# The last fill unit in the scores' banks, the last reciprocal ahead of a weight piece, the last output in halves

## The chip, the core and the metric

One core of one Trainium2 chip runs the whole program. The metric is the time of an execution on the device in microseconds (us), as the median of several runs. TensorE (PE, with its weight loads as PEld), VectorE (DVE), ScalarE (ACT) and GpSimd (POOL) each work through a list of instructions in order; SyncE (SP) issues most of the loads and stores. Engines wait for one another by semaphores alone.

## The reference, cut to what matters

Three blocks follow one another in float32: soft-capped attention, a gated MLP with a spatial gate, and an MLP with a convolution gate.

```python
# attention: B, H, S, D = 2, 12, 448, 64
scores = cap * np.tanh(scale * q @ k.T / cap)
attn = np.exp(scores - max) / (sum + 1e-09)
x = attn @ v                               # to (B, S, 768)
# gated MLP: 768 -> 1024 -> 768
h = gelu(x @ w_in); u, v = h[..., :512], h[..., 512:]
v_s = w_sg @ layernorm(v, g_ln) + b_sg     # over the sequence
x = x + (u * v_s) @ w_out
# convolution gate: 768 -> 1024 -> 768, three taps along the sequence
h = relu(x @ w2_in)
out = (h * sigmoid(conv3(h, conv_w))) @ w2_out
```

## The kernel before, in words

Everything is held transposed: features on the 128 partitions, the 448 positions of a batch along the free side. A product is kept near float32 by splitting both factors into a high and a low part and issuing three matmuls (hi·hi, hi·lo, lo·hi) per tile of 128 features; `mm3` (L110) does this, so a unit over 6 feature tiles is 18 matmuls.

**Attention** (L286) runs over 12 head pairs N in two halves each, so over rounds R of 0 to 26. A round issues scores into four PSUM banks (tile "sc" of the pool `psa`), tanh and exp on ScalarE, and with a lag the products with V and the sums of the exponentials into three banks (tile "pv", named `sums`). That makes seven of the eight banks; the eighth belongs to the pool `psm`, whose one tile "mo" everything shares that takes turns there. All of attention's matmuls go through `ordered` (L383), which pins each behind the one before, so their order is that of the code. `pin(lasta)` and `pin(lastv)` do the same on ScalarE and VectorE for the instructions that use them. Everything else is put in order by a scheduler that is given the program in the order of the code.

**Fill units.** The next stage begins with u units: unit (b, i) is 128 features of x @ w_in for batch b, then a gelu (`gelu`, L221: a square on ScalarE, L223; L226 on VectorE; a tanh on ScalarE, L227; L230 on VectorE, which is the last to read the bank). The first four, of batch 0, are issued inside attention where TensorE would wait: the table `FILL` (L38) says in which round, L637 to L647 issue them. The first takes turns in rounds 15 to 23, the others come whole in rounds 24, 25 and 26. Units 0, 2 and 3 lie in the bank of `psm`; unit 1 lies in bank 1 of a tile "fi" (L642), which takes the four score banks when no more scores are to come.

**The last head pair.** `norm_pe` (L582) divides the last pair by its sums without a round trip through memory: ScalarE copies products and sums out of the banks (L586), VectorE adds a guard (L588) and inverts 224 columns (L589). A step later `spread` (L591) repeats the inverted sums over the partitions with four matmuls (eight passes in the trace, "pv<-E,sel"), VectorE multiplies (L599), and the result is split into X.

**Weights** come as pieces of float64. A piece in attention is loaded by SP, ScalarE or VectorE turns its top words into `hd` (L151, L153), VectorE joins them with the low words (L156), makes the high part (L162) and subtracts it to get the low part (L165). Pieces of later stages go through L181 and L184 on ScalarE, L191 and L194 on VectorE, then L198 and L203; the buffer of a piece is loaded again when its L203 is done.

**The next stage** (`rest`, L728) opens a pool `ps1` of seven banks in the place of the scores' and products' banks. Its units are numbered n: 0 to 3 are the fill units, 4 to 6 v units of batch 0 (matmuls L772 to L774, 512 columns, each followed by a gelu and a layer norm), 7 to 10 u units of batch 1, 11 to 14 v units, 15 to 22 the spatial gate (its product is read by L823, "gt", and split to GH and gl), 23 to 34 the output product. `bank(n)` (L751) says which pool a unit's bank comes from: n below 4 and every fourth from `psm`, the others from `ps1`. The last stage has 16 h units and then 12 output units: `f_unit` (L946) sums 24 matmuls in a bank, ScalarE copies it to `o` with the factor 0.5 (L952) and SP stores it (L953).

Of the kernel before, what the change touches and what calls it, by code (L numbers as in the profile page):

```python
# [9 lines left out]
F32 = mybir.dt.float32  # L10
# [5 lines left out]
AF = mybir.ActivationFunctionType  # L16
ALU = mybir.AluOpType
PSUM = bass.MemoryType.PSUM

P = 128  # L20
B, H, S, D = 2, 12, 448, 64
NPAIR = H // 2
DM, DF, DH = 768, 1024, 512
NK = DM // P
# [3 lines left out]
HS = S // 2  # L28
# [25 lines left out]
def stages(  # L54
# [17 lines left out]
    nc = tc.nc  # L72
    V, A, T, G = nc.vector, nc.scalar, nc.tensor, nc.gpsimd

    now = [0]
    lasta, lastv, lastr, lasts = [None], [None], [None], [None]

    def pin(last):
        return tc.issue_after(last[0].ins) if last[0] is not None else ExitStack()

    def sync(dst, src):

        if lasts:
            with pin(lasts):
                lasts[0] = nc.sync.dma_start(dst, src)
        else:
            nc.sync.dma_start(dst, src)
# [3 lines left out]
    def later(k, fn):  # L91
        due.setdefault(now[0] + k, []).append(fn)
# [7 lines left out]
    def f(ap):  # L100
        return ap.bitcast(F32)
# [19 lines left out]
    psm = ctx.enter_context(tc.tile_pool(name="psm", bufs=1, space=PSUM))  # L121
# [10 lines left out]
    ub = [c0]  # L132

    heads = []

    def decode_half(hi, lo, src, pool, bufs, wait, hi_eng, top_eng):

        n = src.shape[1]
        r = pool.tile([P, 512, 2], U32, tag="f64", name="f64", bufs=bufs)[:, :n]
        words = r.rearrange("p c w -> p (c w)").bitcast(U16)  # L140
        sync(words[:, : 4 * n - 1], src.rearrange("r c w -> r (c w)").bitcast(U16)[:, 1:])
        low = r[:, :, 0]
        top = words.rearrange("p (c w) -> p c w", w=4)[:, :, 2].bitcast(BF16)
        heads.append(heads.pop(0))
        hd = heads[-1][:, :n]

        def s1():
            half = hd.bitcast(F16).rearrange("p (c w) -> p c w", w=2)[:, :, 1]
            with pin(lasta), pin(lastv):
                if top_eng == "a":  # L150
                    A.activation(half, top, AF.Copy)  # L151
                else:
                    V.tensor_copy(half, top)  # L153

        def s2():
            V.scalar_tensor_tensor(  # L156
                out=low, in0=low, scalar=13, in1=hd, op0=ALU.logical_shift_right, op1=ALU.bitwise_or
            )
            if hi_eng == "a":
                A.activation(hi, f(low), AF.Copy)  # L160
            else:
                V.tensor_copy(hi, f(low))  # L162

        def s3():
            V.tensor_tensor(out=lo, in0=f(low), in1=f(hi), op=ALU.subtract)  # L165

        for k, fn in zip(wait, (s1, s2, s3)):
            later(k, fn)
# [106 lines left out]
    def attention(att, psa):  # L275
# [306 lines left out]
        def norm_pe(N, both):  # L582

            b, p = divmod(N, NPAIR)
            both_e = att.tile([P, 2 * (S + HS)], F32, tag="E", name="E", bufs=3)[:, S + HS :]
            A.activation(both_e, both, AF.Copy)  # L586
            e, r = both_e[:, :S], both_e[:, S:]
            V.tensor_scalar(out=r, in0=r, scalar1=guard, scalar2=None, op0=ALU.add)  # L588
            V.reciprocal(out=r, in_=r)  # L589

            def spread():  # L591
                rp = sums[:, :S]
                for c in range(2):
                    for h in range(2):
                        ordered(
                            rp[h * D : (h + 1) * D, c * S // 2 : (c + 1) * S // 2],
                            lhsT=sel[:, 2 * h + c], rhs=r, start=True, stop=True,
                        )
                V.tensor_tensor(out=e, in0=e, in1=rp, op=ALU.mult)  # L599
                split(e, X[:, 0, p, b], X[:, 1, p, b], "a")  # L600

            later(1, spread)

        NN = B * NPAIR
        fill = {}
        done = 0
        for R in range(2 * NN + LAGS[1] + 1):
            N, half = divmod(R, 2)
            if R == 23:
                columns(att)  # L610
            if R == 4:
                load_vlast(3, NN)
            for j, at in enumerate(WIN):
                if at == R:
                    top_eng = "v" if R < 11 else "a"
                    wdec(*wi_piece(w_in, j // NK, j % NK), att, 4, hi_eng="v", wait=(5, 6, 7), top_eng=top_eng)
            if R < 2 * NN:
                if half == 0 and N + 2 < NN:
                    load(N + 2)
                if half == 0 and N + 1 < NN:  # L620
                    load_v(N + 1)
                if R == 1:

                    start_values(0)
                    scores(N, half)
                    value(0, 0)
                    value(0, 1)
                else:
                    scores(N, half)
                if R == 2:  # L630
                    values(0, 0, True)
                    done += 1
                if half == 0 and N + 1 < NN:
                    with pin(sm0) if N == 1 else ExitStack():
                        prep_q(N + 1)
                        prep_k(N + 1)
            if R in FILL:  # L637

                i, k0, k1 = FILL[R]
                if k0 == 0:  # L640
                    if i == 1:
                        free = psa.tile([P, 4, 512], F32, tag="sc", name="fi", bufs=1)  # L642
                    fill[i] = free[:, i, :S] if i == 1 else psm.tile([P, 512], F32, tag="mo", name="mo")[:, :S]
                for k in range(k0, k1):
                    mmw(fill[i], 0, i, k, ordered)
                if k1 == NK:
                    u_done(0, i, fill[i])  # L647
            tick()
            if R > 1 and done < 2 * NN and R - done >= LAGS[R >= LAGS[2]]:
                values(*divmod(done, 2))  # L650
                done += 1
            tick()
# [75 lines left out]
    def rest():  # L728
        cwt = const.tile([P, 3 * NF], F32, name="cwt")
        V.tensor_tensor(out=cwt, in0=f(cw[:, 0]), in1=f(cw[:, 1]), op=ALU.add)  # L730
        ps1 = ctx.enter_context(tc.tile_pool(name="ps1", bufs=7, space=PSUM, reuse_waits="tile"))
        with ExitStack() as s1:
# [16 lines left out]
                G.tensor_copy(XS[:, :, :, b * D : (b + 1) * D], f(X[:, :, :, b, ST:S]))  # L749

            def bank(n):  # L751
                return (psm if n < 4 or n % 4 == 3 else ps1).tile([P, 512], F32, tag="mo", name="mo")

            ub.append(c1)

# [151 lines left out]
        with ExitStack() as s2, ExitStack() as last:  # L907
# [38 lines left out]
            def f_unit(b, m):  # L946
                ps = ps1.tile([P, 512], F32, tag="mo", name="mo")[:, :S]
                c = slice(m * P, (m + 1) * P)
                for i in range(NF):
                    mm3(ps, W2[:, 0, i, c], W2[:, 1, i, c], HG[:, 0, i, b], HG[:, 1, i, b], i == 0, i == NF - 1)  # L950
                o = c2.tile([P, S], F32, tag="cv", name="o", bufs=2)
                A.activation(o, ps, AF.Copy, scale=0.5)  # L952
                nc.sync.dma_start(outT[c, b * S : (b + 1) * S], o)  # L953

# [112 lines left out]
```

## Time and profile before

| | |
|---|---|
| median of 3 runs (lowest, highest) | 327.97 us (326.82, 328.14) |
| the profiled execution's own time | 327.65 us |
| its span, first to last instruction | 325.8 us |
| TensorE busy | 316.0 us, 97% of the span |
| VectorE, ScalarE, GpSimd busy | 242.7, 219.8, 36.7 us |
| granted TensorE clock, mean | 0.994 |

The profile is of one execution. A timeline lists an engine's instructions by their start; equal neighbours are joined with a count, and brackets give the idle time ahead of one and what ended it. Matmuls follow each other before the one ahead has ended, and their ends are modelled, so from start to start is the cost of one.

### The profile page before, as it was taken

How to read it: one execution, taken by the hardware profiler on the slowest of the kernel's cores; microseconds unless marked ns; L12 is line 12 of the kernel's file. 1: busy time of each engine (PE TensorE's matmuls, PEld its weight loads, DVE VectorE, ACT ScalarE, POOL GpSimd, SP SyncE). 2: the span in 40 equal slices, each digit the busy share in tenths (PEclk: the TensorE clock that was granted, in tenths of full speed). 3: DMA queues.
4: the chain of work that ended last, by engine and by line, in shares of the span. 5: the costliest groups of instructions: out<-in, count | busy, mean ns of one | idle time of the engine just before them, and what ended most of it. 6: DMA issues, size and time to landing. Idle time of an engine off the chain costs nothing.

```text
span 325.8 us, 6295 instructions
## 1 busy us (share of the span) xinstructions
PE 316.0 (97%) x2382; PEld 261.6 (80%) x2382; DVE 242.7 (75%) x485; ACT 219.8 (67%) x353; POOL 36.7 (11%) x73
## 2 busy tenths in 40 slices
PE   8998999999999999999999999999999999999992
PEld 6565666666677789988999899999999999999991
DVE  4546998398666899999987979996888999990000
ACT  3998999898973457767565745455777988883010
POOL 4000134051322220211111000000000000000000
PEclk9999999999999999999999999999999999999997
DMA  3488775855423154122213670002391123013211
GB/s 111 117 216 222 243 214 141 222 155 182 156 90 119 58 161 116 52 60 103 66 64 129 198 303 0 2 0 65 112 367 40 32 66 97 1 58 117 84 58 36
DMA packets 22223, 37.75 MB, mean 116 GB/s; under 512 B 7352, under 2 KB 14536, under 8 KB 22184
## 3 DMA queue, kind: packets, MB, share of 16 engines
q1 hardware_dynamic: 20392, 34.51, 34.6%
q0 software_dynamic: 1632, 2.61, 2.7%
q8 instruction: 21, 0.34, 0.4%
q14 instruction: 18, 0.15, 0.2%
q10 hardware_dynamic: 160, 0.13, 0.1%
HBM read 34.40 MB, written 2.79 MB: 114 GB/s over the span
## 4 chain that ended last, share of the span: by engine, by line
PE 70%; DVE 10%; DMA 9%; ACT 6%; issue 2%; SPq 1%; POOL 0%; ACTq 0%; DVEq 0%; POOLq 0%
PE mo L111 14%; PE mo L113 14%; PE mo L112 14%; PE pv L386 11%; PE sc L386 7%; DMA f<-in_w_in_dram 5%; PE mo L386 4%; DMA kr<-in_kT_dram 2%; PE wps L359 1%; ACT raw L403 1%; PE fi L386 1%; PE mo L772 1%; DVE f L191 1%; ACT f L184 1%; PE mo L773 1%
## 5 line engine op out<-in xcount | busy, mean ns | idle before, releaser
L112 PE MATMUL mo<-X,WI 128*128 128x448 f32 x120 | 43.7, 365 | 0.0
L113 PE MATMUL mo<-X,WI 128*128 128x448 f32 x120 | 43.7, 365 | 0.0
L111 PE MATMUL mo<-X,WI 128*128 128x448 f32 x120 | 43.0, 365 | 0.0
L412 ACT ACTIVATE raw<-raw 128x1344 f32<-128x1344 f32 (+2 forms) x25 | 36.4, 1462 | 0.7
L403 ACT ACTIVATE raw<-sc 128x1792 f32<-128x1792 f32 (+1 forms) x22 | 32.4, 1475 | 3.9 <-PE sc L386 3.7
L113 PE MATMUL mo<-HG,W 128*128 128x448 f32 x96 | 34.7, 365 | 0.0
L112 PE MATMUL mo<-HG,W 128*128 128x448 f32 x96 | 34.6, 365 | 0.0
L111 PE MATMUL mo<-HG,W 128*128 128x448 f32 x96 | 33.3, 365 | 0.0
L386 PE MATMUL pv<-raw,V 128*32 128x224 f32 x576 | 32.9, 358 | 0.0
L181 ACT ACTIVATE f<-f 128x256 f32<-128x256 f32 (+2 forms) x44 | 22.8, 517 | 12.9 <-DMA f<-in_w_in_dram 8.1
L191 DVE SCALAR_TENSOR_TENSOR f<-f 128x256 uint32<-128x256 uint32 (+2 forms) x44 | 22.4, 518 | 9.3 <-ACT f L184 8.9
L386 PE MATMUL sc<-Q,K 64*128 64x448 f32 x210 | 27.6, 385 | 0.7 <-ACT raw L403 0.6
L386 PEld LDWEIGHTS pv<-raw,V 128*32 128x32 f32 x576 | 18.8, 109 | 11.5 <-issue 5.5
L386 PEld LDWEIGHTS sc<-Q,K 64*128 64x128 f32 x210 | 18.0, 184 | 10.0 <-ACT raw L403 5.2
L111 PEld LDWEIGHTS mo<-X,WI 128*128 128x128 f32 x120 | 22.5, 188 | 1.9
L112 PEld LDWEIGHTS mo<-X,WI 128*128 128x128 f32 x120 | 22.5, 188 | 1.9
L113 PEld LDWEIGHTS mo<-X,WI 128*128 128x128 f32 x120 | 22.5, 188 | 1.8
L184 ACT ACTIVATE f<-f 128x256 uint32<-128x256 uint32 (+2 forms) x44 | 22.5, 512 | 0.0
L194 DVE SCALAR_TENSOR_TENSOR f<-f 128x256 uint32<-128x256 uint32 (+2 forms) x44 | 22.4, 515 | 0.1
L952 ACT ACTIVATE o<-mo 128x448 f32<-128x448 f32 x12 | 6.3, 542 | 22.8 <-PE mo L113 19.0
L112 PEld LDWEIGHTS mo<-HG,W 128*128 128x128 f32 x96 | 18.0, 188 | 1.4
L111 PEld LDWEIGHTS mo<-HG,W 128*128 128x128 f32 x96 | 18.0, 188 | 1.4
(155 smaller groups left out, 695.5 us busy)
## 6 DMA issues: line engine op xcount, KB each, us to landing
f<-in_w_in_dram SPq DMA_DIRECT2D x12, 512.0 KB, 4.2
f<-in_w_out_dram SPq DMA_DIRECT2D x24, 256.0 KB, 4.8
f<-in_w_in_dram SPq DMA_DIRECT2D x12, 511.8 KB, 5.7
f<-in_w_out_dram SPq DMA_DIRECT2D x8, 384.0 KB, 3.1
qr<-in_qT_dram SPq DMA_DIRECT2D x24, 112.0 KB, 3.0
out_dram<-o SPq DMA_DIRECT2D x12, 224.0 KB, 2.0
rb<-d POOLq DMA_DIRECT2D x22, 112.0 KB, 3.2
V<-in_vL_dram SPq DMA_DIRECT2D x12, 192.0 KB, 3.0
```

The costliest lines, as they stand in the source:

```text
L111: matmul(ps, lhsT=whi, rhs=xhi, start=start, stop=False)
L112: matmul(ps, lhsT=whi, rhs=xlo, start=False, stop=False)
L113: matmul(ps, lhsT=wlo, rhs=xhi, start=False, stop=stop)
L181: A.activation(f(h), f(h), AF.Copy, scale=2.0**-112)
L184: A.activation(l, l, AF.Copy, scale=0.93 * 2.0**-29)
L191: V.scalar_tensor_tensor(out=l, in0=h, scalar=3, in1=l, op0=ALU.logical_shift_left, op1=ALU.bitwise_or)
L194: V.scalar_tensor_tensor(out=l, in0=h, scalar=0x80000000, in1=l, op0=ALU.bitwise_and, op1=ALU.bitwise_or)
L359: T.matmul(wps, lhsT=wz[:, :P], rhs=wz, start=True, stop=True)
L386: lastm[0] = T.matmul(*args, **kw)
L403: lasta[0] = A.activation(x, ps, AF.Tanh, **sc)
L412: lasta[0] = A.activation(x, x, AF.Exp, scale=creg)
L952: A.activation(o, ps, AF.Copy, scale=0.5)
```

## The change

Three edits, in three places.

1. Unit 3, the last fill unit, goes into bank 3 of the tile "fi" and no longer into the bank of `psm` (L643). `bank(n)` gives the bank of `psm` to n = 4 also.
2. ScalarE's copy in `norm_pe` is pinned behind the last pinned ScalarE instruction, and the joining step of every weight piece that comes later (`s2` in `decode_half`, L156) is pinned behind the reciprocal.
3. The last output unit's bank is copied in two halves, ScalarE's and VectorE's, which ScalarE's queue and SP store.

```diff
 def decode_half(...)
         def s2():
-            V.scalar_tensor_tensor(
-                out=low, in0=low, scalar=13, in1=hd, op0=ALU.logical_shift_right, op1=ALU.bitwise_or
-            )
+            with pin(drain):
+                V.scalar_tensor_tensor(
+                    out=low, in0=low, scalar=13, in1=hd, op0=ALU.logical_shift_right, op1=ALU.bitwise_or
+                )
 def norm_pe(N, both)
-            A.activation(both_e, both, AF.Copy)
+            with pin(lasta):
+                lasta[0] = A.activation(both_e, both, AF.Copy)
             e, r = both_e[:, :S], both_e[:, S:]
             V.tensor_scalar(out=r, in0=r, scalar1=guard, scalar2=None, op0=ALU.add)
-            V.reciprocal(out=r, in_=r)
+            drain[0] = V.reciprocal(out=r, in_=r)
 in attention's loop over R
-                    fill[i] = free[:, i, :S] if i == 1 else psm.tile([P, 512], F32, tag="mo", name="mo")[:, :S]
+                    fill[i] = free[:, i, :S] if i % 2 else psm.tile([P, 512], F32, tag="mo", name="mo")[:, :S]
 def bank(n)
-                return (psm if n < 4 or n % 4 == 3 else ps1).tile([P, 512], F32, tag="mo", name="mo")
+                return (psm if n < 5 or n % 4 == 3 else ps1).tile([P, 512], F32, tag="mo", name="mo")
 def f_unit(b, m)
+                if b == B - 1 and m == NK - 1:
+                    A.activation(o[:, :HS], ps[:, :HS], AF.Copy, scale=0.5)
+                    V.tensor_scalar(out=o[:, HS:], in0=ps[:, HS:], scalar1=0.5, scalar2=None, op0=ALU.mult)
+                    nc.scalar.dma_start(outT[c, b * S : b * S + HS], o[:, :HS])
+                    nc.sync.dma_start(outT[c, b * S + HS : (b + 1) * S], o[:, HS:])
+                    return
```

Since the scheduler orders what is not pinned, the lists of the engines change from the handover on. The rows below are such lists; a name's number tells tiles apart.

TensorE at the handover before: mo_1389 is fill unit 2, mo_1449 unit 3, mo_1561 the first v unit (unit 4).

```order
L386 MATMUL mo_1389<-X_75,WI0_76 128x448 x18
...
L386 MATMUL mo_1449<-X_75,WI0_76 128x448 x18
L386 MATMUL pv_169<-E_1434,sel_153 64x224 x4
L772 MATMUL mo_1561<-WI1_77,X_75 128x512
L773 MATMUL mo_1561<-WI1_77,X_75 128x512
L774 MATMUL mo_1561<-WI1_77,X_75 128x512
```

And now: fi_1333 is the tile that holds unit 1 and unit 3, mo_1560 unit 4, mo_1588 unit 5.

```order
L388 MATMUL mo_1389<-X_75,WI0_76 128x448 x18
...
L388 MATMUL fi_1333<-X_75,WI0_76 128x448 x18
L775 MATMUL mo_1560<-WI1_77,X_75 128x512
L776 MATMUL mo_1560<-WI1_77,X_75 128x512
L777 MATMUL mo_1560<-WI1_77,X_75 128x512
...
L388 MATMUL pv_169<-E_1434,sel_153 64x224 x4
L775 MATMUL mo_1560<-WI1_77,X_75 128x512
L776 MATMUL mo_1560<-WI1_77,X_75 128x512
L777 MATMUL mo_1560<-WI1_77,X_75 128x512
L775 MATMUL mo_1588<-WI1_77,X_75 128x512
```

Unit 3 has left the bank of unit 2, and the spread stands behind twelve matmuls of unit 4, not ahead of them all. The list then has units 5 and 6, and behind these units 8, 9, six matmuls of 10, all of 7, and the rest of 10; before it had 7, 8, 9 and 10 in a row.

VectorE at the same place before, from the gelu's end of unit 2 (u_1447) to the gelu of unit 3 (g0_1468); E_1434 holds the last pair's products and sums, f64_1273 is a weight piece.

```order
L230 SCALAR_TENSOR_TENSOR u_1447<-g0_1408,mo_1389 128x448
L156 SCALAR_TENSOR_TENSOR f64_1271<-f64_1271,hd0_139 128x24
L156 SCALAR_TENSOR_TENSOR f64_1273<-f64_1273,hd1_140 128x512
L162 CAST WI1_77<-f64_1273 128x512
L588 TENSOR_SCALAR E_1434<-E_1434,one_72 128x224
L165 TENSOR_TENSOR cw_74<-f64_1271,cw_74 128x24
L165 TENSOR_TENSOR WI1_77<-f64_1273,WI1_77 128x512
L589 RECIPROCAL E_1434<-E_1434 128x224
L730 TENSOR_TENSOR cwt_1518<-cw_74 128x24
L226 SCALAR_TENSOR_TENSOR g0_1468<-g0_1468,mo_1449 128x448
```

And now:

```order
L232 SCALAR_TENSOR_TENSOR u_1447<-g0_1408,mo_1389 128x448
L591 TENSOR_SCALAR E_1434<-E_1434,one_72 128x224
L592 RECIPROCAL E_1434<-E_1434 128x224
L158 SCALAR_TENSOR_TENSOR f64_1271<-f64_1271,hd0_139 128x24
L158 SCALAR_TENSOR_TENSOR f64_1273<-f64_1273,hd1_140 128x512
L167 TENSOR_TENSOR cw_74<-f64_1271,cw_74 128x24
L164 CAST WI1_77<-f64_1273 128x512
L733 TENSOR_TENSOR cwt_1517<-cw_74 128x24
L167 TENSOR_TENSOR WI1_77<-f64_1273,WI1_77 128x512
L228 SCALAR_TENSOR_TENSOR g0_1467<-g0_1467,fi_1333 128x448
```

The guard and the reciprocal have moved from behind the piece's joining and high part to ahead of the piece.

VectorE in the next stage, before, from unit 4's layer norm on (gs_1608 is unit 5; the g0 and u rows are of units 8 and 9):

```order
L801 SCALAR_TENSOR_TENSOR VN_1533<-gs_1580,mv_1610,VN_1533 128x512
L226 SCALAR_TENSOR_TENSOR g0_1759<-g0_1759,mo_1740 128x448
L786 TENSOR_SCALAR mv_1658<-mv_1658 128x1
L793 SCALAR_TENSOR_TENSOR gs_1608<-gs_1608,mv_1658,gbc_73 128x512
L230 SCALAR_TENSOR_TENSOR u_1771<-g0_1731,mo_1712 128x448
L191 SCALAR_TENSOR_TENSOR f64_1708<-f64_1708 128x384
```

And now (gs_1607 is unit 5, mo_1620 unit 6, mo_1666 unit 7, mo_1711 unit 8):

```order
L796 SCALAR_TENSOR_TENSOR gs_1607<-gs_1607,mv_1657,gbc_73 128x512
L228 SCALAR_TENSOR_TENSOR gs_1639<-gs_1639,mo_1620 128x512
L228 SCALAR_TENSOR_TENSOR g0_1685<-g0_1685,mo_1666 128x448
L804 SCALAR_TENSOR_TENSOR VN_1532<-gs_1607,mv_1657,VN_1532 128x512
L228 SCALAR_TENSOR_TENSOR g0_1730<-g0_1730,mo_1711 128x448
L232 SCALAR_TENSOR_TENSOR gs_1639<-gs_1639,mo_1620 128x512
L232 SCALAR_TENSOR_TENSOR u_1735<-g0_1685,mo_1666 128x448
```

The gelu of unit 7 now stands ahead of unit 8's, whose matmuls come first on TensorE.

VectorE's last rows now, with the semaphores that each waits for; o_3406 is the last output.

```order
L205 TENSOR_TENSOR W2_2421<-f64_3169,W2_2421 128x256 [waits Activation_49]
L205 TENSOR_TENSOR W2_2421<-f64_3171,W2_2421 128x256 [waits Activation_49]
L957 TENSOR_SCALAR o_3406<-mo_3381 128x224 [waits DMAHW5_49,DMAHW3_49,DMAHW7_49,DMAHW1_49,Activation_49]
L1005 TENSOR_LOAD one_72 [waits DVE_49]
L1013 COMPARE_AND_BRANCH
```

The half copy waits for ScalarE and for earlier transfers; a wait for TensorE is not among them.

## Rows read from the trace of the kernel before

**Rows 1.** The page, part 1: busy time, share of the span, instructions
```profile
PE 316.0 (97%) x2382; PEld 261.6 (80%) x2382; DVE 242.7 (75%) x485; ACT 219.8 (67%) x353; POOL 36.7 (11%) x73
```

**Rows 2.** Stretches: busy us of PE, PEld, DVE, ACT, POOL; PEclk; DMA; GB/s
```profile
120.00:160.00 40.00, 40.00 (x188) 34.94 (x188) 38.21 (x76) 27.78 (x53) 5.33 (x7) 1.00 0.29 83
160.00:200.00 40.00, 39.92 (x196) 36.40 (x195) 33.62 (x62) 22.50 (x40) 1.81 (x2) 1.00 0.43 146
200.00:319.60 119.60, 119.56 (x590) 110.32 (x588) 85.51 (x176) 74.01 (x169) 0.20 (x4) 1.00 0.22 75
319.60:325.80 6.20, 0.00 (x0) 0.00 (x0) 0.00 (x0) 0.54 (x1) 0.00 (x0) 0.70 0.13 45
```

**Rows 3.** Timeline of PE, handover: start us, us, instruction, count, [idle before]
```profile
99.49 0.60 PE L386 MATMUL pv<-sm,ones 128*32 128x224 f32 x8
100.02 3.94 PE L386 MATMUL mo<-X,WI 128*128 128x448 f32 x18
103.90 0.61 PE L386 MATMUL pv<-raw,vlast 64*64 64x224 f32 x8
...
105.22 0.96 PE L386 MATMUL pv<-raw,ones 128*32 128x224 f32 x16
106.58 3.94 PE L386 MATMUL mo<-X,WI 128*128 128x448 f32 x18 [0.40 <-DVE u L230]
110.62 0.98 PE L386 MATMUL pv<-E,sel 128*64 128x224 f32 x8
111.53 0.50 PE L772 MATMUL mo<-WI,X 128*128 128x512 f32 x1
```

**Rows 4.** Timeline of DVE, the same stretch
```profile
105.91 0.62 DVE L230 SCALAR_TENSOR_TENSOR u<-g,mo 128x448 f32<-128x448 f32 x1 [0.64 <-ACT g L227]
106.44 0.94 DVE L156 SCALAR_TENSOR_TENSOR f<-f,hd 128x24 uint32<-128x24 uint32 x2
...
108.00 0.32 DVE L588 TENSOR_SCALAR E<-E,one 128x224 f32<-128x224 f32 x1
...
108.94 1.54 DVE L589 RECIPROCAL E<-E 128x224 f32<-128x224 f32 x1
110.40 0.11 DVE L730 TENSOR_TENSOR cwt<-cw 128x24 f32<-128x24 f32 x1
111.14 0.62 DVE L226 SCALAR_TENSOR_TENSOR g<-g,mo 128x448 f32<-128x448 f32 x1 [0.62 <-ACT g L223]
...
112.41 0.62 DVE L230 SCALAR_TENSOR_TENSOR u<-g,mo 128x448 f32<-128x448 f32 x1
```

**Rows 5.** Timeline of ACT, the same stretch
```profile
105.78 0.89 ACT L151 ACTIVATE hd<-f 128x24 f16<-128x24 bf16 x2
106.53 0.71 ACT L586 ACTIVATE E<-pv 128x672 f32<-128x672 f32 x1
```

**Rows 6.** Timeline of all engines, from the last matmul on
```profile
319.64 0.54 ACT L952 ACTIVATE o<-mo 128x448 f32<-128x448 f32 x1 [4.32 <-PE mo L113]
320.21 0.33 SPq L953 DMA_DIRECT2D out_dram<-o  x1
```

**Rows 7.** Timeline of PE: first matmul of two u units in a row
```profile
123.92 0.36 PE L111 MATMUL mo<-X,WI 128*128 128x448 f32 x1
...
127.58 0.36 PE L111 MATMUL mo<-X,WI 128*128 128x448 f32 x1
```

**Rows 8.** Timeline of DVE at 136 us and at 180 us
```profile
136.28 0.74 DVE L793 SCALAR_TENSOR_TENSOR gs<-gs,mv,gbc 128x512 f32<-128x512 f32 x1
...
180.33 0.69 DVE L191 SCALAR_TENSOR_TENSOR f<-f 128x512 uint32<-128x512 uint32 x1 [0.66 <-ACT f L184]
180.94 0.62 DVE L823 TENSOR_TENSOR gt<-mo,u 128x448 f32<-128x448 f32 x1
```

**Rows 9.** Waits in 160 to 200 us: total us, times, longest
```profile
PEld mo L111 <- DVE gt L823: 0.5, 1, 0.5
```

**Rows 10.** Landing of the stores of o (tile o), us
```profile
DMA to landing us min/median/max: 1.9/2.0/3.9
```

More of the change, by code (lines that the diff above doesn't have):

```diff
@@ L134, in stages @@
     heads = []
+    drain = [None]
     def decode_half(hi, lo, src, pool, bufs, wait, hi_eng, top_eng):
```

## Prediction

> **What bounds the kernel now.** I read the page first: TensorE is busy 316.0 of 325.8 us [rows 1], so a change is worth what it takes out of TensorE's idle time or off the two ends. The table of stretches says where idle time is left [rows 2]: in 120 to 160 us TensorE is full, in 160 to 200 it lacks 0.08 us, in 200 to 319.6 it lacks 0.04, and after 319.6 there are 6.2 us with no matmul. The granted clock is 1.00 (the 2.4 GHz level) up to 319.6 us; the 0.70 behind it lies where no matmul runs. Then I read TensorE's own timeline where attention hands over to the next stage [rows 3]. The fourth fill unit (18 matmuls at 106.58) waits for "DVE u L230", the last reader of the one bank that it shares with the third unit. Behind it stand the eight passes that spread the last sums (110.62) and the first v unit (111.53). The timelines of VectorE and ScalarE over the same stretch [rows 4, 5] show who is late: u L230 ends at 105.91 + 0.62 = 106.53, and the reciprocal of the last sums ends at 108.94 + 1.54 = 110.48, because the decoding of a weight piece (two L156 and what follows) stands ahead of it. The tail is a chain [rows 6]: the last copy, its store, the landing.
>
> **Part 1, the fourth fill unit in the scores' banks.** What would the handover cost without the wait? In the same timeline a group of pv matmuls (99.49 + 0.60 = 100.09) is followed by a fill unit at 100.02, 0.07 us ahead of the group's modelled end [rows 3]. The last group before the fourth unit ends at 105.22 + 0.96 = 106.18, so the unit would start at 106.11 and not at 106.58: **0.47 us** gained. It goes into bank 3 of the tile whose bank 1 the second fill unit used, and its X and the rows of its weights served the units before it, so nothing else is late there.
>
> The spread also waited. A fill unit gives way to pv matmuls 0.06 us ahead of its modelled end (100.02 + 3.94 = 103.96, next at 103.90); the fourth ends at 110.52, so the spread could have come at 110.46 and came at 110.62: **0.16 us**. In the new order twelve matmuls of the v unit stand ahead of the spread. A fill unit takes 103.90 - 100.02 = 3.88 us to its successor, so the v unit starts at 109.99, and at (123.92 - 111.53)/54 = 0.229 us a matmul [rows 3, 7] the spread comes at 109.99 + 12 x 0.229 = 112.74. With both gains the three v units end at 123.29 and not at 123.92. From there to 319.6 us TensorE has next to no idle time to give back, so **0.63 us** is what this part can bring.
>
> **Part 2, the reciprocal ahead of the piece's work.** ScalarE's copy of the last sums (L586, 0.71 us) no longer stands behind two hd copies of 0.89 us [rows 5]; the sums are complete at 106.18, so it ends near 106.89. L588 and L589 follow on VectorE (0.32 + 1.54 [rows 4]) and end near 108.75, against 110.48. With the spread at 112.74 the cover is 4.0 us, and even the old 110.48 would be in time there: in this order the part costs and brings nothing by itself. If the spread stood right behind the fill unit (109.99), it would be worth 0.5 us. What it delays is the piece: the block from L156 to L730 took 106.44 to 110.51, 4.07 us, of which L588 and L589 are 1.86; the other 2.21 now end near 111.0. The thirteenth v matmul needs that piece at 112.74 + 0.91 (the spread, 110.62 to 111.53) = 113.65. That leaves 2.6 us.
>
> **The new wait of part 1.** The second v unit takes the first bank of the pool that replaces the scores' banks, and its first matmul waits for VectorE: the tile of the fill units is free only after the fourth unit's L230. VectorE is clear near 111.0; L226, tanh and L230 take the 1.89 us that they take now (111.14 to 112.41 + 0.62 [rows 4]), so the bank is free near 112.9. TensorE arrives at 113.65 + 3 x 0.229 = 114.3. I cost it at nothing; the cover is 1.4 us.
>
> **What the bank rule moves.** Unit 4 takes the single bank, so unit 7 (a u unit that uses it too) must wait for unit 4's gelu, and the order now issues it after units 8, 9 and a third of 10. A u unit takes 127.58 - 123.92 = 3.66 us [rows 7], so it starts at 123.29 + 2 x 3.66 + 1.22 = 131.83, its last matmul ends 3.94 later as in rows 3, and ScalarE's square of 0.54 us makes it 136.4 with the handovers. On VectorE its L226 stands right behind the L226 of unit 6. Before, VectorE had finished the L793 of unit 5 at 136.28 + 0.74 = 137.02 [rows 8]; four gelu instructions that were ahead of that point are now behind it and one is ahead. At 0.62 each [rows 4] VectorE would arrive near 137.02 - 1.86 = 135.2 and stand for **1.2 us**. It is busy 38.21 of 40 us there, but idle for 6.4 us in the next 40 [rows 2], so I take this as absorbed, and price the opposite as a rival.
>
> In 160 to 200 us TensorE's loads waited once, 0.5 us for "DVE gt L823" [rows 9]; that gt, at 180.94, stood behind L191 of a weight piece that came late [rows 8]. Now two gt stand ahead of that L191. Up to 0.5 us could come back; with VectorE possibly late I take 0, and keep the 0.5 for the range.
>
> **Part 3, the last output in halves.** No row shows a copy of half a unit from a bank. ScalarE: 448 columns take 0.54 [rows 6], 672 take 0.71 [rows 5], so 224 columns less are 0.17 less: 0.37 us. VectorE: L588 on 224 columns takes 0.32, and 448 columns from a bank take 0.62 [rows 4]; these are the bounds, and I take 0.32 for the equal size. The order lists a wait for ScalarE, and none for TensorE, at VectorE's half, so it starts when ScalarE's half is done. A handover to SP is 320.21 - 319.64 - 0.54 = 0.03, so the last store goes out 0.37 + 0.03 + 0.32 + 0.03 = 0.75 us after the copy's start. Now that is 0.57 [rows 6]: **0.18 us lost**. Side by side it would be 0.35, and 0.22 gained. ScalarE's own store (issue 0.33 us, as SP's) is out before that. A landing of half the bytes can be as long as one of all; I leave it.
>
> The Trainium skill bears on this one point ("PSUM — Partial Sum Buffer", section "PSUM bank collisions raise a hardware error"): two engines must not touch one bank on the same partitions at a time, reads against reads included, and disjoint columns don't help. By that rule the wait is forced and the tail is 0.18 us longer, not 0.22 shorter. The trace of before does not show two engines reading one bank at a time, so no row confirms it.
>
> **Sum.** -0.47 - 0.16 + 0.18 = -0.45 us. The profiled execution took 327.65 us (span 325.8), 0.32 below the median of 327.97 of the runs shown. Taken off the median: **327.5 us**. A difference under 0.5% (1.6 us) can't be told from none here.
>
> **Rivals.**
> - A, the halves run side by side (the listed wait is for something older): -0.63 - 0.22 gives 327.1. For it: the two halves have an engine and a store queue each. Against it: VectorE lists no wait for TensorE, so ScalarE's half must be what stands for the last matmul. 0.08.
> - B, VectorE's 1.2 us are not regained and reach the place where TensorE had no margin, the gt near 181 us. Then TensorE is held until 1.2 us after the old time, whatever was gained earlier: +1.2 + 0.18 gives 329.35, slower than before as soon as any of the lateness is left there. If VectorE stands so a second time it is 330.5. For it: 38.21 of 40 us busy and the 0.5 us wait. Against: 6.4 us idle behind it, and gt moved ahead of the piece. 0.21.
> - C, the last store lands as the others do. It took 3.9 us, the longest of the twelve; the median is 2.0 [rows 10]. If all of the 1.9 us comes off the end, -0.45 - 1.9 gives 325.6. Nothing in the change aims at it, a store split over two queues can as well meet the same delay, and something else may end as late as the landing. 0.09.
> - D, the gain at 106 us is lost again at the next wait and the 0.18 stays: 328.15. Against it: TensorE is full behind it, so a new wait would have to appear, such as the one for the fill tile, which has 1.4 us. 0.07.
>
> **Numbers.** The forecast has 0.55. Its own bounds are 327.0 (the 0.5 comes back) to 327.8 (VectorE's half at 0.62 us). Some 80% are held by 326.2 to 329.2: D and the lower part of B are in, B's upper part and C are out. Faster by over 0.5% is most of C and a little for causes not seen, 0.09; slower by over 0.5% is the upper part of B, 0.10; the rest 0.81.
>
> **What would show it.** Right: no wait at the fourth fill unit's first matmul, the spread behind twelve v matmuls without idle time, v units that end 0.6 us earlier, VectorE standing near 136 us before an L226, its half copy starting after ScalarE's has ended, and the last SP store 0.2 us later behind the last matmul. Wrong: a matmul that waits near 114 us for the fill tile (D), TensorE idle for more than 0.5 us between 160 and 200 us (B), the two halves starting together (A), or a last landing near 2 us with a tail shorter by more than 1 us (C).

## The result and the profile after

The changed kernel took **331.05 us** (median of four runs, 330.41 to 333.69) against 327.74 us for the kernel before in the same comparison (four runs, 326.82 to 328.14). The ratio is 1.0117 [1.0083, 1.0151]: slower by 1.2%. The forecast was 327.5 us, and its range ended at 329.2. The profiled execution of the changed kernel took 330.41 us with a span of 328.6 us, 2.8 us more than the span of 325.8 before. Its line numbers are higher by one to nine: L191, L198, L203, L226 and L800 of before are L193, L200, L205, L228 and L803 here.

The page, part 1, which answers to [rows 1]:

```profile
PE 317.0 (96%) x2382; PEld 261.6 (80%) x2382; DVE 243.6 (74%) x486; ACT 219.4 (67%) x353; POOL 40.6 (12%) x73
```

The same stretches as in [rows 2], the later ones moved by 2.4 us (the last matmul ends 2.48 us later):

```profile
120.00:160.00 40.00, 40.00 (x188) 35.03 (x187) 36.14 (x71) 25.70 (x50) 7.12 (x8) 1.00 0.26 75
160.00:200.00 40.00, 38.53 (x186) 34.53 (x186) 34.94 (x64) 22.98 (x41) 2.95 (x2) 1.00 0.46 155
200.00:322.00 122.00, 121.38 (x597) 111.66 (x595) 87.12 (x179) 74.82 (x170) 0.20 (x4) 1.00 0.22 73
322.00:328.60 6.60, 0.04 (x1) 0.00 (x0) 0.39 (x1) 0.36 (x1) 0.00 (x0) 0.80 0.14 45
```

TensorE is still full from 120 to 160 us, but VectorE did 2.07 us less work in this stretch than before (36.14 for 38.21) and ScalarE 2.08 less: they fell behind while nothing of it showed on TensorE. TensorE's idle time is in 160 to 200 us (1.47 us where 0.08 was) and behind 200 us (0.62).

The handover came out as drawn. TensorE's timeline, against [rows 3], shows the fourth fill unit (now "fi") and the v unit without idle time, and the spread behind twelve matmuls:

```profile
105.47 0.96 PE L388 MATMUL pv<-raw,ones 128*32 128x224 f32 x16
106.36 3.94 PE L388 MATMUL fi<-X,WI 128*128 128x448 f32 x18
110.14 0.39 PE L775 MATMUL mo<-WI,X 128*128 128x512 f32 x1
...
112.97 0.98 PE L388 MATMUL pv<-E,sel 128*64 128x224 f32 x8
```

When the starts of equally numbered matmuls are compared between the two traces, the changed kernel is 0.25 us late ahead of the handover (both do the same there) and 0.33 early behind it: 0.58 us gained. It keeps that until 164 us, is 1.88 late at 178, 1.53 late from 190 to 264, and 2.48 late from 274 to the end. The tail adds 0.36. So the span's 2.8 us are made up of 0.25 ahead of the handover, -0.58 at it, +2.23 near 167 us, -0.35 near 181, +0.91 near 272 and +0.36 behind the last matmul. The waits of TensorE in 110 to 322 us name two places (VN is the layer-normed v, GH and gl the high and low part of its gated product, HG the gated tile of the last stage, which the output units read):

```profile
PEld mo L111 <- ACT VN L803: 1.5, 1, 1.5
PEld mo L112 <- DVE gl L108: 1.1, 2, 0.8
...
PEld mo L111 <- ACT HG L107: 1.0, 1, 1.0
```

The gl and VN waits are near 167 us; they cost 2.2 us together. HG is at 272 us. The chain of the changed kernel, in order of time (start, us, what), shows what ended the VN wait:

```profile
164.49 0.60 DVE f L193
165.09 0.61 DVE f L196
165.70 0.02 issue
165.72 0.68 ACT WI L200
166.40 0.05 issue
166.46 2.04 POOL mv L792
168.50 0.02 issue
168.52 0.73 ACT VN L803
169.25 0.04 issue
169.30 0.47 PE mo L111
```

Before, the chain in this stretch is TensorE alone. VectorE is busy without a gap ahead of the pow, and the pow on GpSimd (POOL mv L792) took 2.04 us, where its other six took 0.92 to 1.00. Where VectorE fell behind is in the timelines of VectorE and ScalarE (brackets: idle before):

```profile
148.39 1.09 ACT L225 ACTIVATE gs<-mo 128x512 f32<-128x512 f32 x2 [2.86 <-PE mo L777]
...
149.02 1.29 DVE L228 SCALAR_TENSOR_TENSOR gs<-gs,mo 128x512 f32<-128x512 f32 x2 [1.93 <-ACT gs L225]
```

ScalarE waited 2.86 us for unit 11, VectorE 1.93 us for ScalarE. Such a wait with nothing else done is called a stand below. TensorE's list is 8, 9, part of 10, 7, the rest of 10, then 12, eight matmuls of 13, 11, the rest of 13, 14; ScalarE's and VectorE's lists still have the gelu of 11 ahead of that of 12.

The tail, timeline from the last matmul on:

```profile
322.12 0.36 ACT L956 ACTIVATE o<-mo 128x224 f32<-128x224 f32 x1 [4.03 <-PE mo L113]
322.51 0.36 ACTq L958 DMA_DIRECT2D out_dram<-o  x1
322.51 0.39 DVE L957 TENSOR_SCALAR o<-mo 128x224 f32<-128x224 f32 x1 [26.86 <-ACT o L956]
322.93 0.33 SPq L959 DMA_DIRECT2D out_dram<-o  x1
```

VectorE's half starts when ScalarE's is done, so the last store is issued 322.93 - 322.12 = 0.81 us after the copy's start; before it was 0.57 [rows 6].

### The profile page after: what moved, and what is told of

It reads as the page before. It is cut to its first block, busy times and chain, and to the rows that moved or that the text cites. A ratio compares the mean times of both kernels' runs of the same rounds, so it can differ in the third digit from the quotient of the medians.

```text
span 328.6 us, 6292 instructions
## 1 busy us (share of the span) xinstructions
PE 317.0 (96%) x2382; PEld 261.6 (80%) x2382; DVE 243.6 (74%) x486; ACT 219.4 (67%) x353; POOL 40.6 (12%) x73
## 4 chain that ended last, share of the span: by engine, by line
PE 74%; DMA 6%; ACT 5%; DVE 5%; SPq 5%; issue 2%; POOL 1%; DVEq 0%; ACTq 0%
PE mo L111 14%; PE mo L112 13%; PE mo L113 13%; PE pv L388 13%; PE sc L388 7%; SPq L85 4%; PE mo L775 3%; PE mo L776 3%; PE mo L777 3%; PE mo L388 2%; PE fi L388 2%; DMA f<-in_w_out_dram 2%; DMA kr<-in_kT_dram 2%; DMA f<-in_w_in_dram 1%; DVE cv L930 1%
## 5 line engine op out<-in xcount | busy, mean ns | idle before, releaser
L193 DVE SCALAR_TENSOR_TENSOR f<-f 128x256 uint32<-128x256 uint32 (+2 forms) x44 | 23.0, 532 | 8.5 <-ACT f L186 8.2
L196 DVE SCALAR_TENSOR_TENSOR f<-f 128x256 uint32<-128x256 uint32 (+2 forms) x44 | 23.0, 528 | 0.2
```

Of the source, the lines that this page charges most:

```text
L193: V.scalar_tensor_tensor(out=l, in0=h, scalar=3, in1=l, op0=ALU.logical_shift_left, op1=ALU.bitwise_or)
L196: V.scalar_tensor_tensor(out=l, in0=h, scalar=0x80000000, in1=l, op0=ALU.bitwise_and, op1=ALU.bitwise_or)
```

## The experiments

Every ratio is to the kernel before in the same comparison.

| kernel | median us (lowest to highest) | ratio [95%] |
|---|---|---|
| e1, edit 1 alone | 332.19 (332.04 to 333.0) | 1.0143 [1.0101, 1.0185] |
| e2, edit 2 alone | 327.56 (326.93 to 328.9) | 0.9996 [0.9974, 1.0018] |
| e3, edit 3 alone | 328.49 (327.57 to 329.53) | 1.0016 [0.9993, 1.0038] |
| e4, edits 1 and 2 | 330.47 (330.05 to 332.0) | 1.0088 [1.0058, 1.0118] |
| e5, only the bank rule | 331.19 (329.61 to 334.44) | 1.0108 [1.0049, 1.0167] |
| e6, only the fill unit's place | 327.57 (326.95 to 329.4) | 0.9980 [0.9954, 1.0006] |
| e7, the change, units in turn | 328.01 (327.1 to 329.57) | 1.0009 [0.9990, 1.0028] |
| e8, e7 without the halves | 327.61 (327.15 to 329.49) | 1.0001 [0.9979, 1.0022] |
| e9, the change, loads in order | 330.42 (329.44 to 331.44) | 1.0072 [1.0046, 1.0098] |
| e10, e8 with loads in order | 326.98 (326.19 to 327.83) | 0.9956 [0.9932, 0.9979] |
| e12, the change, gl's other form | 331.47 (331.22 to 333.93) | 1.0131 [1.0064, 1.0198] |
| e13, the change, no wait for the pow | 333.03 (330.2 to 334.64) | 1.0132 [1.0066, 1.0199] |
| e14, e13 with loads in order | 331.01 (329.96 to 333.36) | 1.0106 [1.0066, 1.0145] |

**Which edit: e1 to e4.** Each is the kernel before with the hunks of the named edits of the change. In these four texts T1 is that the units out of turn (edit 1) do the harm, T2 that the pins of edit 2 do, T3 that the tail does; later texts say what theirs are.

> Edit 1 alone (unit 3 in the scores' banks, unit 4 in the single bank), without the pinned reciprocal and without the halves. Theory T1, the bank rule's turn does the harm: units 7 and 11 are issued out of turn on TensorE while ScalarE and VectorE keep their gelus ahead of units that are done earlier, so the layer norms come late and TensorE stands near 166 to 170 us. Then this run is slower than before by 1.5 to 3.5 us (329.3 to 331.3), with a stand of 1 us or more for a layer-normed tile (VN) between 160 and 180 us, and its handover ends about 0.6 us early. Rival T2, the pins of edit 2 do the harm by holding back weight pieces: then this run is 0.3 to 0.8 us faster than before.

> Edit 2 alone (copy pinned, decoding of the later pieces behind the reciprocal). The order of the matmuls is that of before. T1: within 0.4 us of before; the reciprocal ends about 1.7 us earlier and the spread no longer waits (0.16 us gained at most). T2: slower by 1 us or more, with late weight pieces.

> Edit 3 alone (last output in halves). T1: the span from the end of the last matmul to the end of the program grows by 0.2 to 0.4 us (6.23 before, 6.59 in the changed kernel); the time is within 0.6 us of before. Rival T3, the tail carries the loss: slower by 1 us or more.

> Edits 1 and 2, the last output whole again. T1: as slow as the changed kernel less 0.2 to 0.4 us, so about 2.5 to 3 us above before, with the same stand for VN between 165 and 170 us. T3: as fast as before or faster.

Edit 1 carries the loss: by itself it loses no less than the whole change (the intervals overlap). Its 332.19 us lie above T1's range, which ended at 331.3. Edit 2 leaves TensorE's list as it was and changes nothing that can be measured. Edit 3 alone costs 0.16%, which isn't clear of noise, but its tail grew by 0.71 us where T1 had 0.2 to 0.4. e1 stands near 167 us as the changed kernel does (1.1 us for gl in two waits, 1.5 for VN), and in its profile something is added behind that stand. Its stretches:

```profile
168.00:170.00 2.00, 0.91 (x4) 0.70 (x4) 2.00 (x5) 1.54 (x3) 0.43 (x1) 0.93 0.00 0
170.00:174.00 4.00, 4.00 (x14) 3.55 (x14) 3.97 (x9) 1.37 (x3) 0.36 (x1) 0.61 0.58 169
```

The granted clock falls to 0.61 as a mean of 170 to 174 us. From 169.78 to 172.76 us matmuls start every 0.373 us and not every 0.204 (the 1.2 GHz level), which makes TensorE 1.5 us later. In the profiled executions of the change, e4 and e12 the same stand was followed by 1.00; e9's profile has the fall again (0.65 in 170 to 174 us).

The halves: seven traces with them end 6.59 to 7.13 us behind the last matmul (median 6.84), eight without 6.16 to 6.40 (median 6.32). So they cost about 0.5 us, of which 0.24 is the later issue and the rest lies behind it.

**Which half of edit 1: e5 and e6.**

```diff
 e5, in bank(n) of before
-                return (psm if n < 4 or n % 4 == 3 else ps1).tile(...)
+                return (psm if n < 5 or n % 4 == 3 else ps1).tile(...)
 e6, in attention's loop of before
-                    fill[i] = free[:, i, :S] if i == 1 else psm.tile(...)
+                    fill[i] = free[:, i, :S] if i % 2 else psm.tile(...)
```

> Before with one word changed: bank(n) gives the single bank to unit 4 as well. The fourth fill unit stays in the single bank, so the 0.6 us at the handover are not gained, and TensorE's list has the later units out of turn (7 behind 8, 9 and a part of 10; 11 behind 12 and a part of 13). T1 (the units out of turn make the layer norms late): 329 to 332 us, TensorE standing for 1 to 2 us between 160 and 180 us, ended by VN. T2 (the fourth fill unit's new place does the harm, by the tile that two gelus must free): 327.7, no stand.

> Before with the other word changed: the fourth fill unit in bank 3 of the scores' tile, bank(n) as before. The units 7 to 14 are issued in turn. T1: 327.1 to 328.0 us: the handover's gain of 0.4 to 0.6 us less a possible short wait for the fill tile near 114 us, and no stand over 0.5 us between 160 and 180 us. T2: 329 to 332.

The bank rule alone gives the whole loss; the fill unit's new place costs nothing that can be measured. In e5 TensorE's list has 7 and 11 out of turn, VectorE stands 1.80 us and ScalarE 2.66 us near 148 us. e5's waits of TensorE in 160 to 322 us:

```profile
PEld mo L111 <- ACT HG L107: 1.9, 1, 1.9
PEld mo L112 <- DVE gl L108: 1.8, 3, 0.6
...
PEld mo L111 <- ACT VN L800: 0.3, 1, 0.3
```

The pow took 0.90 us here and VN hardly held TensorE (T1 had VN end a stand of 1 to 2 us), yet TensorE is 1.86 us later at 190 us than at 164: 0.63 lost near 167 and 1.5, for gl and GH, at 184 to 187, less 0.25 regained between. The stands near 148 us were as long as in the change, and their price came out at other places. e6 shows why the rule was changed with the place: unit 4 then takes the fill tile's first bank and waits for its gelu, in TensorE's timeline

```profile
113.12 0.50 PE L772 MATMUL mo<-WI,X 128*128 128x512 f32 x1 [0.42 <-DVE u L230]
```

TensorE in e6 is 0.52 us late ahead of the handover, 0.04 at the fourth fill unit and 0.39 from 140 us on: of 0.48 us gained 0.35 are lost again.

**The units in turn: e7 and e8.** Up to unit 6 both have the changed kernel's list, then 7 to 14 in turn.

```diff
-                return (psm if n < 5 or n % 4 == 3 else ps1).tile(...)
+                return (psm if n < 5 or (n % 4 == 3 and n > 11) else ps1).tile(...)
```

> The changed kernel, all three edits, with bank(n) giving units 7 and 11 a bank of the seven, so that TensorE issues 7 to 14 in turn; up to unit 6 the list is that of the changed kernel. T1: 327.6 us (before, less 0.6 at the handover, plus 0.4 in the tail), TensorE idle under 0.3 us between 160 and 180 us, all of GpSimd's pow operations near 0.9 us or, if one of them is 2 us, without a stand behind it. T3 (the late layer norm comes from what the handover moved on VectorE, not from the turn of the units): 330 to 331, with the same stand near 167 us.

> As the run before, without the halves: the last output unit is copied and stored whole. T1: 327.2 us, tail 6.2 to 6.3 us behind the last matmul; 0.2 to 0.5 less than with the halves. T3: 330.0 to 330.5.

No stand near 167 us in either, and all pows take 0.90 to 1.00 us. In e7 TensorE gains 0.60 us at the handover and another 0.34 near 181 us, where [rows 9] had a wait of 0.5; it gives 0.37 back at 270 us for HG and 0.60 in the tail. So the units' turn is shown to cause VectorE's stand at 148 us and TensorE's at 167, while the kernel is no faster than before: something near 270 us remains, and it is 0.62 us in e8.

**The stand near 272 us: e9 and e10.** In the changed kernel ScalarE waits for a piece of the last weight matrix, and so does everything behind it in the chain to HG. ScalarE's timeline near 240 us:

```profile
240.41 0.44 ACT L183 ACTIVATE f<-f 128x256 f32<-128x256 f32 x1 [3.96 <-DMA f<-in_w_out_dram]
```

Before, that wait was 2.29 us and ended at 235.43. SP's list tells why: when the last stage's pool opens, the third and fourth pieces, which ScalarE needs first, stand second and fourth among the loads before, fifth and seventh in the changed kernel, e1, e4 and e5, fourth and sixth in e6 to e8. The edit pins them ahead:

```diff
 in sync(dst, src), outside attention
-            nc.sync.dma_start(dst, src)
+            with pin(hold):
+                loads.append(nc.sync.dma_start(dst, src))
+    hold, loads = [None], []
 in w2_piece(), n being the piece's number
+                    hold[0] = loads[3 - n] if n >= 6 and loads else None
                     wdec(W2, w2_out, *pieces.pop(0), *stage, wait=(1, 1, 1), cols=256, low_eng="a")
+                    hold[0] = None
```

> The changed kernel with one addition: the loads of the third and fourth piece of the last weight matrix are pinned ahead of the loads into the pool that opens in the last stage, so SP's list has them first there and not fifth and seventh. T-load (the stand of TensorE near 272 us, ended by HG, comes from SP's order of these loads, which the edit's rescheduling changed: the third piece lands 6.1 us after its buffer is free, against 3.0 before): ScalarE's wait for that piece near 236 us falls from 4.0 to 2 us or less, no stand over 0.2 us near 272 us, time 330.1 us (0.95 less); the stand near 167 us stays. Rival (the stand near 272 us is the same lateness of VectorE and ScalarE as at 167 us, carried on): the stand stays, 331.

> Fill unit in the scores' banks, reciprocal first, units 7 to 14 in turn, the loads in the better order, the last output whole. T-load with T1: neither the stand near 167 us nor the one near 270 us (0.6 us in the run in turn), so 327.0 us, 0.6 to 0.8 below before, and a span of 325.1. Rival (the handover's gain is lost at another wait further on): 327.6 or more.

ScalarE's wait in e9:

```profile
236.68 0.44 ACT L185 ACTIVATE f<-f 128x256 f32<-128x256 f32 x1 [1.06 <-DMA f<-in_w_out_dram]
```

No matmul waits for HG any more, so the order of the loads is the cause of that stand. The median of 330.42 us is 0.63 below the change's, where T-load had 0.95; the intervals of the two ratios overlap, so here the trace decides and not the time. e9's profiled execution (331.09 us) has the clock's fall behind 169 us; whether its other executions have it no trace shows. e10, with both causes and the halves taken away, is the only kernel here that beats the one before clear of noise, 0.9956 [0.9932, 0.9979]: TensorE is 0.61 us earlier behind the handover, and 0.8 us ahead of the trace of before from 190 to 264 us. Its stretch from 160 to 200 us:

```profile
160.00:200.00 40.00, 40.00 (x198) 36.67 (x197) 33.65 (x62) 23.44 (x43) 1.82 (x2) 1.00 0.43 142
```

The profiled execution, 327.83 us, is the longest of e10's twelve, and its end shows why its trace alone would not prove the gain. From 272 us to the last matmul its matmuls start every 0.207 us and not every 0.203, with the granted clock at 1.00, and TensorE ends 0.24 us later than before. e4's and e5's profiles have the same, the others do not, and no run shows what it comes from. From 280 to 300 us, e10 first, then before:

```profile
280.00:300.00 20.00, 20.00 (x98) 18.18 (x97) 12.32 (x31) 13.66 (x35) 0.00 (x0) 1.00 0.17 62
280.00:300.00 20.00, 20.00 (x101) 18.54 (x100) 12.49 (x32) 13.36 (x35) 0.00 (x0) 1.00 0.17 62
```

**GpSimd's pow: e11 to e14.** Is the pow of 2.04 us half of the stand near 167 us? e11 is a small kernel of its own.

```diff
+for kind in KINDS:
+    ...
+    issue(lambda: V.tensor_scalar(out=m, in0=m, scalar1=1.0, scalar2=None, op0=ALU.add))
+    G.tensor_tensor(out=m, in0=m, in1=nh, op=ALU.pow)
+    ...
+    issue(lambda: V.tensor_scalar(out=z[:, 0:1], in0=m, scalar1=0.0, scalar2=None, op0=ALU.mult))
```

> Nothing of the kernel but GpSimd's pow on one column, fourteen times, each beside six VectorE instructions of one kind: none; two SBUF operands; one SBUF operand; one SBUF and one PSUM operand; the first and the last of these in turn; the subtraction of pieces; the joining of words. It computes none of the outputs. T-port (VectorE instructions with two SBUF operands, back to back, keep GpSimd from its operands until they are through; it explains the 2.03 us of the pow at 166.46): beside six instructions with two SBUF operands the pow takes 3.5 us or more, ending with the last of them; 0.9 to 1.0 alone, beside one operand, and beside PSUM; in turn with PSUM operands 1.0 to 1.7. Rival (the pow waits for the semaphore of another engine, or the trace's end is wrong): 0.9 to 1.0 in every group.

GpSimd's timeline, the first seven in the order of the expectation (the second seven are the same):

```profile
4.73 0.55 POOL L69 TENSOR_TENSOR mv<-mv,nh 128x1 f32<-128x1 f32 x1 [4.29 <-DVE mv L68]
5.61 0.93 POOL L69 TENSOR_TENSOR mv<-mv,nh 128x1 f32<-128x1 f32 x1 [0.33 <-DVE mv L68]
9.34 2.34 POOL L69 TENSOR_TENSOR mv<-mv,nh 128x1 f32<-128x1 f32 x1 [2.80 <-DVE mv L68]
12.01 0.55 POOL L69 TENSOR_TENSOR mv<-mv,nh 128x1 f32<-128x1 f32 x1 [0.33 <-DVE mv L68]
15.71 0.92 POOL L69 TENSOR_TENSOR mv<-mv,nh 128x1 f32<-128x1 f32 x1 [3.16 <-DVE mv L68]
19.43 3.14 POOL L69 TENSOR_TENSOR mv<-mv,nh 128x1 f32<-128x1 f32 x1 [2.79 <-DVE mv L68]
22.90 0.93 POOL L69 TENSOR_TENSOR mv<-mv,nh 128x1 f32<-128x1 f32 x1 [0.33 <-DVE mv L68]
```

and VectorE's beside the second, third and sixth:

```profile
5.45 3.69 DVE L46 SCALAR_TENSOR_TENSOR d<-a,b 128x512 f32<-128x512 f32 x6
...
9.18 2.09 DVE L49 TENSOR_SCALAR d<-a 128x512 f32<-128x512 f32 x6
...
19.27 2.89 DVE L60 TENSOR_TENSOR d<-a,b 128x384 f32<-128x384 f32 x6
```

A pow can be held by VectorE, but not as expected (so, other than said ahead of the prediction, not every wait of an engine for another is one for a semaphore). Six tensor_scalar or six tensor_tensor in a row hold it until 0.41 us behind the last (9.34 + 2.34 against 9.18 + 2.09); six scalar_tensor_tensor on two SBUF operands let it in behind the first (it ends 0.41 us behind that one's end), and beside PSUM operands it takes the 0.55 us that it takes alone. Both theories' numbers missed in part. So the suspect was the one TENSOR_TENSOR near the pow at 166.46, the one that makes gl. e12 gives it the other form:

```diff
-lastv[0] = split(t, GH[:, i, b], GL[b, i], "a")
+A.activation(GH[:, i, b], t, AF.Copy)
+lastv[0] = V.scalar_tensor_tensor(out=GL[b, i], in0=t, scalar=1.0, in1=f(GH[:, i, b]),
+                                  op0=ALU.mult, op1=ALU.subtract)
```

> The changed kernel; only the instruction that makes gl on VectorE (L108, out of gt and GH) takes another form: the subtraction is issued as a scalar_tensor_tensor with the factor 1. All five engines' lists stay as they are, row for row. T-port (the pow at 166.46 took 2.03 us because VectorE's TENSOR_TENSOR on gl, back to back behind L796, kept GpSimd from its operands, and 1.1 of the 1.9 us that TensorE loses near 167 us are this): the pow takes 0.9 to 1.0 us, the layer norm comes 1.1 us earlier, TensorE stands about 0.3 us and not 1.45 for it, and the time is 330.0 us. Rival 1 (the order of the units alone makes the layer norm late, the pow has slack): pow 0.9, stand and time unchanged, 331. Rival 2 (the pow is long for a cause that is not gl's form): 2.0 us again, 331.

```profile
165.93 2.03 POOL L792 TENSOR_TENSOR mv<-mv,one 128x1 f32<-128x1 f32 x1 [7.42 <-ACT WI L200]
```

The pow took 2.03 us again, and the time was 331.47: rival 2. Last, the pow is taken off the chain with every list as it is:

```diff
-A.activation(hi, g[r], AF.Copy, scale=mv[r, 1:2])
+A.activation(hi, g[r], AF.Copy, scale=nhalf[r])
 ...
-    out=lo, in0=g[r], scalar=mv[r, 1:2], in1=f(hi), op0=ALU.mult, op1=ALU.subtract
+    out=lo, in0=g[r], scalar=nhalf[r], in1=f(hi), op0=ALU.mult, op1=ALU.subtract
```

> The changed kernel; the layer norm's last factor is read from a constant and no longer from the pow's result, in ScalarE's VN and in VectorE's. The pow is still computed and nobody waits for it; the factor of the layer norm is left out. All five lists stay as they are. T-pow (1.1 us of the stand near 167 us are the long pow): ScalarE's VN comes near 167.0 and not at 168.5, TensorE stands 0.75 us for gl and under 0.2 for VN, 329.3 to 329.8 us in all. T-late (VectorE's lateness alone sets the stand, and VN's low part, which VectorE makes, is late in any case): TensorE still stands over 1 us for VN's other part, 330.6 to 331.2.

> The same with the loads of e9 in the better order. T-pow with T-load: what is left is VectorE's lateness itself (0.75 for gl), the halves' 0.4 and the handover's gain of 0.6: 328.0 to 328.6 us, no stand near 272 us. T-late: 329.8 to 330.3.

In e13 ScalarE's VN comes at 166.81 us and TensorE no longer waits for it. But its waits of TensorE in 160 to 200 us are now

```profile
PEld mo L111 <- ACT GH L107: 2.9, 1, 2.9
...
PEld mo L112 <- DVE gl L108: 2.2, 4, 0.8
```

Two of the gl waits are near 167 us, the other two at 184 to 186; GH is at 191, and the sum is larger than in the change. e14 has 2.3 for gl and 2.2 for GH. Its chain names what GH waited for, a weight piece that stands ahead of it on ScalarE:

```profile
181.69 7.46 DMA f<-in_w_in_dram
...
189.23 0.65 ACT f L185
189.88 0.54 ACT f L188
190.42 0.93 ACT GH L109 x2
```

In the changed kernel the load of that piece was issued 1.5 us later, at 183.23 us, and yet landed sooner. Its time from issue to landing, in us:

```profile
DMA to landing us min/median/max: 3.8/3.8/3.8
```

In the traces of before, e1, e4, e5, e7, e9, e10 and e12 it took 4.0 to 5.0 us, in e13 8.05 and in e14 7.46; no run shows why. So T-pow holds for the wait for VN, and its time did not come, but e13 and e14 do not show that the same lateness is merely paid later. Of what TensorE loses at 184 to 192 us in e14, 1.1 us are for gl, for which e5 lost time there too, and the 2.1 us for GH come with the long load. T-late's range of 330.6 to 331.2 missed e13, whose four runs lie between 330.2 and 334.64 (in the profile, 334.64, the clock fell once more, behind the wait of 2.9 us), and its wait for VN's other part did not come. e14, 331.01, is above both of its ranges: taking the pow and the order of the loads out does not bring the time back while the units are out of turn.

## Why the prediction was wrong

- **What bounds the kernel**: right. TensorE has no idle time to give, so the handover's gain stayed a gain (0.58 us in the change, 0.60 in e7; 0.63 was worked out), and every stand behind it is a loss.
- **Part 1's handover, the new wait for the fill tile, part 2**: right. No idle time at 106 us, the spread behind twelve matmuls, the second v unit not held, the reciprocal done at 107.62 + 1.55 = 109.17 us, in a trace 0.25 us late there, against 108.75 worked out. e2 confirms the nothing of part 2 by itself.
- **"What the bank rule moves"** is the step that failed, at the words "I take this as absorbed": a lateness of VectorE was put at nothing in the sum. In its place TensorE lost 2.24 us near 167 us, 0.88 for gl and 1.36 for VN. With the rule alone (e5) the kernel is 1.1% slower, with the units back in turn (e7) it is not. Three things in the step were off. First, only unit 7 was costed. The rule's every fourth unit means that 11 is late for 7 as 7 is for 4, and VectorE's stand was there: none near 136 us, where VectorE was through with unit 6 at 136.44 and not at 135.2, and 1.93 us at 149. Second, the 6.4 us of idle time were counted over 160 to 200 us. What matters is the idle time ahead of the next thing that TensorE takes from VectorE, near 167 us, and up to there VectorE's timeline before has two gaps:

```profile
147.02 0.56 DVE L191 SCALAR_TENSOR_TENSOR f<-f 128x384 uint32<-128x384 uint32 x1 [0.48 <-ACT f L184]
163.98 0.69 DVE L191 SCALAR_TENSOR_TENSOR f<-f 128x512 uint32<-128x512 uint32 x1 [1.71 <-ACT f L184]
```

  of which the second is a wait for ScalarE's work on a weight piece. Third, ScalarE's own stand was not looked for, and it was longer (2.86 us). That the pow then took 2.04 us, 1.1 us longer than the others, could not be read from the rows, and its cause is open.
- **The gt near 181 us**: the 0.5 us did come back in part, 0.35 in the change and 0.34 in e7; they were taken as 0 and kept for the range.
- **Part 3**: mechanism right, size off. VectorE's half took 0.39 us (0.32 was taken) and the issue moved by 0.24 (0.18 worked out), and about 0.3 us more lie behind the issue by the medians of the traces (0.12 in the change's own), which "I leave it" left out. The two halves follow one another: ScalarE's takes 0.36 us from 322.12, VectorE's starts at 322.51 and was released by it. By the Trainium skill ("PSUM — Partial Sum Buffer", section "PSUM bank collisions raise a hardware error") two engines must not read one bank on the same partitions at a time; the trace agrees in so far as they don't.
- **Rival B** had the mechanism, VectorE's lateness held against TensorE, with 0.21. Its place was the gt at 181 us and its price 1.2; it was paid at 167 us, 2.2, and a second time at 272. Its "twice" value of 330.5 is near the result by luck: the second payment was not VectorE's, since the scheduler had also moved SP's loads of the last stage, over 100 us behind the edit. No step of the prediction looked at SP's list there. A, C and D did not occur.
- **The chances** gave 0.10 to slower by over 0.5%. That followed from the step above: B was held down by the 6.4 us of idle time, of which 4.7 lie behind 167 us.

## What to carry to other kernels

When an edit makes one unit wait for a buffer, follow the turn of every later unit that shares the buffer, and compare the producer's order with the order in which the consumers have their lists: a consumer that keeps the old order stands for the late unit while later ones lie ready. Look for the idle time that could absorb a helper engine's lateness ahead of the next thing that the bounding engine takes from it, not behind. And compare the lists of all queues to the end of the program, the loads too: a scheduler may move them far from the edit, and here undoing that by a pin turned e8, as fast as before, into e10, faster by 0.4%.

## What the hardware showed that was not expected

- GpSimd's pow on one column took 0.55 us alone and beside scalar_tensor_tensor with a PSUM operand, 0.93 beside scalar_tensor_tensor on two SBUF operands, and as long as the row of VectorE instructions beside tensor_scalar or tensor_tensor (2.34 and 3.14 us, e11). The Trainium skill ("SBUF — State Buffer", section "Who interferes with whom") says that VectorE with two SBUF inputs, or in its two-port modes, contends with a GpSimd instruction that reads SBUF, and that whichever comes second is blocked until the first is through. e11 agrees for single instructions: each held pow ends some 0.41 us behind the end of a VectorE instruction. That a row of some kinds holds GpSimd throughout and a row of others lets it in after one, the runs add.
- What made the pow at 166.46 us long stays open. It ends 0.41 us behind the second next VectorE instruction in the change, e1, e4, e9 and e12; in e5 it had the same neighbours and took 0.90 us.
- After a wait of 1.5 us for VN TensorE's granted clock fell to the 1.2 GHz level for some 3 us in e1 and e9, and stayed at 2.4 GHz in the profiled executions of the change, e4 and e12. Where it fell, in e1, it cost 1.5 us, as much as the wait itself.
- One load of a weight piece took 7.46 and 8.05 us from issue to landing in e14 and e13, and 3.8 to 5.0 us in nine other traces. The cause is open.
